# One load of 128 partitions issued as two, of 120 and of 8, at the start of a retention and Fourier-mix kernel

## The chip, the cores and the metric

The kernel runs on one core of a Trainium2 chip. The metric is the device time of one execution in microseconds; the median of three runs before the change is 243.88 us, with a lowest of 243.7 and a highest of 243.89. The core has a matrix engine (PE, with its weight loads shown as PEld), a vector engine (DVE), a scalar engine (ACT), a general engine (POOL) and a queue engine that only issues transfers (SP). Transfers run on 16 DMA engines that all queues share.

## The reference, cut to what matters

Inputs are `q`, `k` and `v` of 4 batches, 8 heads, 768 positions and 64 columns, and two weight matrices of 512 x 2048 and 2048 x 512. The first half is a linear attention with a decay per head, the second a two-dimensional Fourier mix with a normed feed-forward part:

```python
state = gamma * state + k[:, :, t] (outer) v[:, :, t]        # for every position t
y[:, :, t] = q[:, :, t] @ state / sqrt(64)
x = y, heads side by side                                    # 4 x 768 x 512
u = x + real(fft(fft(x, axis=1), axis=2))
ch = relu(norm(u) @ w_ch1) @ w_ch2
out = u + ch                                                 # 4 x 768 x 512, float32
```

## The kernel before

The work goes batch by batch, and inside a batch by four pairs of heads, in the order of `PAIR_ORDER`. For each pair, `load_unit` (line 162 on) issues three loads of 384 KB on SP's queue, `q`, `k` and `v`, each to one tile of 128 partitions x 2 heads x 6 chunks x 64 columns in float32 (the issue itself is line 171). Pairs are counted from 0, so the first batch's fourth `k` is the load that is called k3 here; its neighbours are q3 and v3. The `q` of the first batch is read in runs of 1536 bytes, `k` and `v` in runs of 256 bytes, twelve to a partition.

For the first batch all twelve loads are issued at the very start, back to back. `first_units` then writes out the order of the first batch by hand. Per pair: POOL casts `q` (`q0_unit`, line 403) and scales `k` (`k0_unit`, lines 412 and 415, both halves on POOL for the first three pairs; for the fourth pair line 412 on POOL and line 419 on ACT), and casts `v` (`v0_unit`, line 428; for the fourth pair the second half is cast by DVE on line 432). PE transposes `q` and `k` (line 444), ACT copies the results out (lines 452 and 455), PE makes the masked products (line 469), DVE masks them (line 476), PE makes the states of the chunks (line 491), DVE scans them (line 500), and PE adds up the output (lines 515 and 531), which ACT writes to the batch's `x` (line 544). Then come DVE's folds (lines 684 and 694), the Fourier products (lines 741, 854, 858) and the feed-forward part (lines 978, 961 and 1000).

Between the cast of q3 and the scaling of k3, POOL issues the first of eight weight transfers (`w1_unit`, line 1154); the other seven (lines 1154 and 1161) follow right behind the cast of v3. `filler` (line 157) puts matmuls on zeros into PE's stream. The second batch's loads wait for the seventh weight transfer and for a matmul of the first batch's feed-forward part.

The order on each engine has two sources. In the first batch every instruction is tied to the one before it on its engine by `pin`, so its order is that of `first_units`. Behind it, the units of all streams are sorted by hand-set due times in `emit`; from then until the last batch only POOL's order in the first stretch is tied:

```python
            if e[0] < 1.0:
                behind()
                pin(None if e[0] < 0.05 else ["Pool", "GpSimd"])
            elif e[0] > B - 1:
                pin()
```

Where nothing is tied, the framework's planner orders the instructions of an engine when the kernel is built, from the order of the code and from its own estimate of when each is ready. The four zero fills of `qt_zeros` (lines 270 and 271) belong to that part: the code has them as one unit.

Of the kernel before, what the change touches and what calls it, by code (L numbers as in the profile page):

```python
# [18 lines left out]
P = 128  # L19
# [30 lines left out]
def kernel(  # L50
# [9 lines left out]
    nc = tc.nc  # L60
# [103 lines left out]
    def load_unit(b, i, after=None):  # L164
        def run():
            h0 = 2 * PAIR_ORDER[i]
            for name, src in srcs.items():
                t = inp.tile([P, 2, NCH, D], f32, tag="in32", name=f"{name}32")
                rows = "h (p c) d -> p h c d" if b < NPE and name == "q" else \
                    "h (c p) d -> p h c d"  # L170
                dma = nc.sync.dma_start(t, src[b, h0:h0 + 2].rearrange(rows, p=P))  # L171
                if after is not None:
                    for x in (w_dma[after].ins, lb[0]["mm"].ins):
                        tc.add_manual_dep(dma.ins, x.name,
                                          mybir.DependencyInfo(mybir.DependencyClass.Sync,
                                                               mybir.DependencyReason.DATA),
                                          reason="loads in turn")
                if b > 1:
                    tc.add_manual_dep(dma.ins, a_of[b - 1, 1].ins.name,
                                      mybir.DependencyInfo(mybir.DependencyClass.Sync,  # L180
                                                           mybir.DependencyReason.DATA),
                                      reason="loads behind the transposes")
                in_of[name, b, i] = t
        return run
# [152 lines left out]
    for j in range(2):  # L337
        x = const.tile([P, NCH, 2, XW], f16, tag=f"x16_{j}", name=f"x16_{j}")
# [5 lines left out]
        t = const.tile([P, 257], f32, tag=f"qn_{j}", name=f"qn_{j}", padded_shape=[P, 260])  # L344
# [1020 lines left out]
```

## Time and profile before

| | |
|---|---|
| median of three runs | 243.88 us (243.7 to 243.89) |
| the profiled execution's own time | 244.0 us |
| its span | 241.8 us |
| granted TensorE clock | 1.0 throughout |
| PE busy | 230.9 us, 95% of the span |
| DVE busy | 193.0 us, 80% |
| ACT busy | 126.5 us, 52% |
| POOL busy | 87.1 us, 36% |
| loads on line 171 | 48, of 384 KB each |

The span is the profiled execution from its first to its last instruction; 2.2 us of the execution's own time lie around it. An engine's row in a timeline gives the start in us, the length in us, the engine, the line, the operation and what it writes and reads; a bracket behind it gives the idle time before it and what ended that. A chain of work is followed back from the last instruction, at each step to what released it. In a row of stretches, each engine has its busy time and, in brackets, how many instructions it began; the last three figures are PE's clock, the mean busy share of the 16 DMA engines (packets that overlap on an engine count twice, so that it can go over 1) and GB/s.

### The profile page before, as it was taken

How to read it: one execution, taken by the hardware profiler on the slowest of the kernel's cores; microseconds unless marked ns; L12 is line 12 of the kernel's file. 1: busy time of each engine (PE TensorE's matmuls, PEld its weight loads, DVE VectorE, ACT ScalarE, POOL GpSimd, SP SyncE). 2: the span in 40 equal slices, each digit the busy share in tenths (PEclk: the TensorE clock that was granted, in tenths of full speed). 3: DMA queues.
4: the chain of work that ended last, by engine and by line, in shares of the span. 5: the costliest groups of instructions: out<-in, count | busy, mean ns of one | idle time of the engine just before them, and what ended most of it. 6: DMA issues, size and time to landing. Idle time of an engine off the chain costs nothing.

```text
span 241.8 us, 5656 instructions
## 1 busy us (share of the span) xinstructions
PE 230.9 (95%) x2160; PEld 155.8 (64%) x2160; DVE 193.0 (80%) x478; ACT 126.5 (52%) x280; POOL 87.1 (36%) x150
## 2 busy tenths in 40 slices
PE   6797899999999999999999999999999999999995
PEld 2354568956676655665567546565567458998884
DVE  8998957898897888996787677899985856768264
ACT  8798669588775435662237522742247305253340
POOL 6667600465600058691000553690000602240302
PEclk9999999999999999999999999999999999999999
DMA  7999999799999567999999758787110141131202
GB/s 172 252 265 146 201 200 202 173 246 236 291 222 228 97 146 167 169 201 126 261 274 222 138 118 234 128 111 173 43 46 0 26 130 43 24 110 24 87 0 89
DMA packets 99466, 36.41 MB, mean 151 GB/s; under 512 B 89840, under 2 KB 96624, under 8 KB 99440
## 3 DMA queue, kind: packets, MB, share of 16 engines
q1 hardware_dynamic: 95072, 31.79, 63.4%
q0 software_dynamic: 4224, 4.19, 10.8%
q8 instruction: 17, 0.28, 0.5%
q10 hardware_dynamic: 144, 0.07, 0.1%
q14 instruction: 9, 0.07, 0.1%
HBM read 27.26 MB, written 6.29 MB: 139 GB/s over the span
## 4 chain that ended last, share of the span: by engine, by line
PE 76%; DVE 6%; SPq 4%; POOL 4%; DMA 3%; ACT 3%; issue 2%; POOLq 0%; ACTq 0%
PE psc L1000 22%; PE psh L961 19%; PE psh L1042 9%; PE psc L1113 7%; SPq L171 4%; PE ps L741 4%; PE wkA L605 3%; DMA q<-in_q_dram 3%; PE psh L978 3%; PE wkY L659 2%; PE wkY L655 2%; PE pq L838 1%; PE wkK L624 1%; PE tq L561 1%; POOL u L877 1%
## 5 line engine op out<-in xcount | busy, mean ns | idle before, releaser
L1000 PE MATMUL psc<-w,ht 128*128 128x512 f16 x288 | 68.3, 379 | 0.0
L961 PE MATMUL psh<-unT,w 128*128 128x384 f16 x320 | 59.5, 326 | 0.0
L875 POOL TENSOR_TENSOR u<-u,x 128x256 f32<-128x256 f32 x21 | 13.5, 643 | 104.9 <-DVE u L845 95.7
L1000 PEld LDWEIGHTS <-ht 128*128 128x128 f16 x288 | 27.1, 98 | 25.7 <-issue 0.2
L961 PEld LDWEIGHTS <-w 128*128 128x128 f16 x320 | 29.9, 98 | 16.0 <-issue 0.6
L965 ACT ACTIVATE ht<-psh 128x384 f16<-128x384 f32 x46 | 22.3, 489 | 24.2 <-PE psh L961 24.0
L608 DVE TENSOR_TENSOR atm<-wkA,maskp 128x512 f16<-128x512 f32 x36 | 23.8, 683 | 1.0 <-PE wkA L605 1.0
L1042 PE MATMUL psh<-unT,w 128*128 128x256 f16 x192 | 21.5, 272 | 0.0
L967 DVE TENSOR_SCALAR ht<-psh 128x384 f16<-128x384 f32 x34 | 18.7, 549 | 2.1 <-PE psh L961 2.1
L895 DVE BATCH_NORM_STATS2 bst<-u 128x6 f32<-128x512 f32 x21 | 14.6, 693 | 7.2 <-POOL u L877 7.1
L1042 PEld LDWEIGHTS <-w 128*128 128x128 f16 x192 | 18.7, 98 | 2.2
L1047 ACT ACTIVATE ht<-psh 128x512 f16<-128x512 f32 x21 | 12.5, 597 | 13.1 <-PE psh L1042 8.2
L634 DVE SCALAR_TENSOR_TENSOR s<-s,gk,wkK 128x128 f16<-128x128 f16 x48 | 16.4, 342 | 2.7 <-ACT s L630 1.9
L1004 DVE SCALAR_TENSOR_TENSOR ob<-psc,stats,u 128x512 f32<-128x512 f32 x18 | 13.4, 744 | 4.9 <-PE psc L1000 4.8
L667 ACT ACTIVATE x<-wkY,gexp 128x384 f16<-128x384 f32 x24 | 12.8, 581 | 8.3 <-PE wkY L659 8.3
L900 ACT ACTIVATE un<-u,stats 128x512 f16<-128x512 f32 x15 | 10.8, 721 | 10.6 <-DVE stats L896 7.1
L388 POOL TENSOR_SCALAR kd<-k,gexp 128x384 f16<-128x384 f32 x24 | 13.9, 590 | 3.8 <-DMA k<-in_k_dram 3.8
L157 PE MATMUL wps<-ht 128*128 128x512 f16 x40 | 12.6, 418 | 2.2 <-POOL ht L208 2.2
L877 POOL TENSOR_TENSOR u<-u,x 128x256 f32<-128x256 f32 x21 | 13.3, 635 | 3.3 <-DVE u L848 2.1
L605 PE MATMUL wkA<-qTz,kT 128*128 128x256 f16 x72 | 13.4, 273 | 0.1
L978 PE MATMUL psh<-unT,w 128*128 128x128 f16 x192 | 11.5, 219 | 0.1
L978 PEld LDWEIGHTS <-w 128*128 128x128 f16 x192 | 11.0, 98 | 0.7 <-issue 0.5
(191 smaller groups left out, 415.6 us busy)
## 6 DMA issues: line engine op xcount, KB each, us to landing
q<-in_q_dram SPq DMA_DIRECT2D x16, 384.0 KB, 6.3
k<-in_k_dram SPq DMA_DIRECT2D x16, 384.0 KB, 5.7
v<-in_v_dram SPq DMA_DIRECT2D x16, 384.0 KB, 6.3
out_dram<-ob SPq DMA_DIRECT2D x18, 256.0 KB, 2.7
w<-in_moe_w_ch_dram POOLq DMA_DIRECT2D x8, 512.0 KB, 10.9
out_dram<-o SPq DMA_DIRECT2D x2, 512.0 KB, 2.9
out_dram<-o SPq DMA_DIRECT2D x3, 128.0 KB, 1.8
unT<-un SPq DMA_TRANSPOSE x15, 2.5
```

The costliest lines, as they stand in the source:

```text
L605: mm = nc.tensor.matmul(wk[:, c2], st["kT"][:, c, :], st["qT"][:, :, c, :], start=True, stop=True)
L608: nc.vector.tensor_tensor(out=st["atm"][:, 2 * part:2 * part + 2], in0=wk, in1=maskp[:, PAIR_ORDER[i]].unsqueeze(1).to_broadcast([P, 2, 2, ...
L634: nc.vector.scalar_tensor_tensor(out=s16[:, c], in0=s16[:, c - 1], scalar=gk2[:, hp:hp + 1], in1=wk[:, c - c0], op0=ALU.mult, op1=ALU.add)
L877: nc.gpsimd.tensor_tensor(out=u[:, kb, 256:512], in0=u[:, kb, 256:512], in1=x[:, kb, 1, 257:1:-1], op=ALU.add)
L895: nc.vector.bn_stats(bst, u[:, kb, :])
L961: nc.tensor.matmul(psh, w116[:, cb, fb * P:(fb + 1) * P], unT[:, cb, rt * 384:(rt + 1) * 384], start=(cb == 0), stop=(cb == 3))
L965: nc.scalar.activation(ht16[:, fb, :], psh, AF.Relu, bias=0.0, scale=-1.0)
L967: nc.vector.tensor_scalar(out=ht16[:, fb, :], in0=psh, scalar1=-1.0, scalar2=0.0, op0=ALU.mult, op1=ALU.max)
L978: mm = nc.tensor.matmul(psh[:, f], w116[:, cb, fb * P:(fb + 1) * P], unT[:, cb, kb * P:(kb + 1) * P], start=(cb == 0), stop=(cb == 3))
L1000: nc.tensor.matmul(psc, ht16[:, fb, rb3 * P:(rb3 + 1) * P], w216[:, fb, :], start=(fb == 0), stop=(fb == NFB - 1))
L1042: nc.tensor.matmul(psh[:, t], w116[:, cb, fb * P:(fb + 1) * P], unT[:, cb, p * 256:(p + 1) * 256], start=(cb == 0), stop=(cb == 3))
L1113: nc.tensor.matmul(ps[:, c0:c1], lh(f), rh(f)[:, c0:c1], start=first and f == 0, stop=last and f == 7, skip_group_check=True)
```

## The change

The load k3, and no other, is issued as two transfers on the same queue, one behind the other: partitions 0 to 119, then partitions 120 to 127. Both write the same tile, so whoever reads the tile waits for both. Nothing else differs.

```diff
                 t = inp.tile([P, 2, NCH, D], f32, tag="in32", name=f"{name}32")
                 rows = "h (p c) d -> p h c d" if b < NPE and name == "q" else \
                     "h (c p) d -> p h c d"
-                dma = nc.sync.dma_start(t, src[b, h0:h0 + 2].rearrange(rows, p=P))
+                x = src[b, h0:h0 + 2].rearrange(rows, p=P)
+                cut = 120 if (b, i, name) == (0, 3, "k") else P
+                dma = nc.sync.dma_start(t[0:cut], x[0:cut])
+                if cut < P:
+                    nc.sync.dma_start(t[cut:P], x[cut:P])
```

## The prediction

> **What bounds the kernel now.** I read the page first: shares of busy time, then the chain that ended last.
>
> ```profile
> PE 230.9 (95%) x2160; PEld 155.8 (64%) x2160; DVE 193.0 (80%) x478; ACT 126.5 (52%) x280; POOL 87.1 (36%) x150
> PE 76%; DVE 6%; SPq 4%; POOL 4%; DMA 3%; ACT 3%; issue 2%; POOLq 0%; ACTq 0%
> ```
>
> PE bounds the kernel as a whole, but the change sits in the first 23 us, and there the chain runs through transfers. So I asked for the chain in order of time around the fourth pair.
>
> ```profile
> 11.71 7.67 DMA q<-in_q_dram
> ...
> 19.55 0.83 POOL q16z L403
> 20.38 0.90 POOL w L1154
> 21.29 0.04 issue
> 21.33 0.98 POOL kd L412
> 22.31 0.13 issue
> 22.44 0.49 PE tq L444 x6
> ```
>
> The reader should see that the chain waits for q3, not for k3: q3 lands at 11.71 + 7.67 = 19.38, POOL casts it, issues a weight transfer, and only then comes to k3. The DMA issues, asked for one at a time, give k3's and v3's landings (us from issue to landing is the last figure), and the timeline gives their starts, POOL's row for v3 and PE's and DVE's rows that need v3.
>
> ```profile
> 14.41 0.47 SPq L171 DMA_DIRECT2D k<-in_k_dram  x1
> 15.00 1.46 SPq L171 DMA_DIRECT2D v<-in_v_dram  x1
> k<-in_k_dram SPq DMA_DIRECT2D x1, 384.0 KB, 6.7
> v<-in_v_dram SPq DMA_DIRECT2D x1, 384.0 KB, 7.5
> 22.53 0.55 POOL L428 TENSOR_SCALAR v<-v 128x384 f16<-128x384 f32 x1 [0.23 <-DMA v<-in_v_dram]
> 23.28 0.54 DVE L432 CAST v<-v 128x384 f16<-128x384 f32 x1
> 24.31 0.47 PE L491 MATMUL wkK<-v,kd 128*64 128x64 f16 x10
> ```
>
> k3 lands at 14.41 + 6.7 = 21.11, which is 0.18 us before POOL is free for it (21.29). v3 lands at 15.00 + 7.5 = 22.5. Last I cut the tail of these loads into stretches; the last two figures are the busy share of the 16 DMA engines and GB/s. A row of the DMA queues for 16.0 to 17.5 us goes with it.
>
> ```profile
> 20.00:20.50 0.50, 0.06 (x1) 0.06 (x2) 0.50 (x2) 0.50 (x3) 0.50 (x2) 1.00 1.31 211
> 21.00:21.50 0.50, 0.50 (x6) 0.26 (x5) 0.50 (x2) 0.50 (x1) 0.46 (x2) 1.00 0.13 34
> 21.50:22.00 0.50, 0.45 (x13) 0.32 (x11) 0.50 (x2) 0.50 (x2) 0.50 (x1) 1.00 0.07 16
> q8 instruction: 1, 0.02, 5.5%
> q1 hardware_dynamic: 66, 0.02, 7.5%
> ```
>
> A share of 0.07 of 16 engines is 1.1 engines: at 21 us nearly all engines are done with all twelve loads, and one is still working through its parts of k3 and v3. The last row is the load queue from 21.0 to 22.0: 66 packets of 256 bytes in 1 us, one every 15.2 ns, one engine's pace. One instruction packet at 16.0 to 17.5 us held one engine for 0.055 x 16 x 1.5 = 1.3 us, which is about the lag. That it is the same engine is my inference; which of the 16 it is, these views don't say.
>
> **The change, part by part.** Three things change: SP issues one more transfer, k3's rows are dealt to the engines in two portions, and the readers of k3 wait for two transfers.
>
> The issue. k3's issue takes 0.47 us and v3's 1.46 us. The nearest rows for an issue of 8 partitions are the k issues, 0.45 to 0.47 us; plus the gap of 0.04 between issues, v3 is issued about 0.5 us later, at 15.5. Its data starts to move behind k3's, at about 19 us or later, so 0.5 us or even another 1.5 us (if the extra issue has to wait as v3's does) hides in the 3.5 us in between. SP issues nothing else until 44.58. Cost 0. Without that cover it would be 0.5 us on v3, of which 24.31 - 23.82 = 0.49 us is slack at PE: DVE's cast of v3's half ends at 23.82, and PE needs it at 24.31.
>
> The portions. Eight rows are 8 x 12 = 96 packets. If a portion of 120 still gives its engines 8 rows each and the 8 rows go one to an engine, an engine with a ninth row has 12 packets more, 12 x 15.2 ns = 0.18 us. Three cases by which engine is the late one: it gets a ninth row, and k3 lands at 21.11 + 0.18 = 21.29, just as POOL comes free; it has eight as before, and k3 lands at 21.11; it has none, and k3 lands with the others, before 20.9, when the share has dropped. The scaling starts at 21.33 in the last two and by 21.42 in the first (0.13 from landing to start, below). Cost 0 to 0.09 us. An early landing brings nothing, because POOL is still at q3 and the weight issue until 21.29, and these follow q3, which is queued ahead of k3 and isn't touched. v3 moves with it: 0.18 later at worst, which is inside the 0.49 us; or, if the late engine is relieved of 96 packets, to about 21.3, when POOL casts it at 22.34 in place of 22.53. Then seven weight issues come 0.19 us earlier. That is worth nothing: the second batch's loads that wait for a weight transfer wait last for a PE matmul of L978 (2.0 us by the waits of SP's queue), and no row of PE's waits names a weight transfer.
>
> [...]
>
> The waits. POOL's line 412 and ACT's line 419 get a second transfer to wait for. The nearest rows: the first pair's scaling, which has a separate semaphore instruction, starts at 6.09 after a landing at 1.32 + 4.6 = 5.92, 0.17 us; the second pair's, without one, starts at 10.68 after 5.04 + 5.6 = 10.64, 0.04 us. So a second wait costs 0.13 us when it comes last and nearer to the 0.04 of a queue step when both are long over. POOL's is on the chain: +0.05 us, between 0 and 0.13. Behind the waiting instruction on POOL stand the cast of v3 and seven weight issues, all covered as above. On ACT, line 419 starts at 21.68 behind a copy that runs until 21.79; it ends at 22.30 and POOL's half at 22.31, and PE needs both. So 0.05 us on ACT falls beside POOL's 0.05 and not on top; without POOL's it would count in full.
>
> The sum: 0 + 0 to 0.09 + 0.05, of which I take 0.05 for likeliest, since two of the three cases cost nothing. The profiled execution's 244.0 becomes 244.05; that execution is 0.12 us above the median of 243.88, so the forecast is 243.9 to 243.95 against the runs, and I name 243.95.
>
> **The rivals.** First, the planner. Behind the first batch most of the order is the planner's, made from estimated times, and an added transfer can shift its estimates. The profile shows that it moves things: the unit of four zero fills stands scattered.
>
> ```profile
> 39.18 0.38 DVE L270 MEMSET qTz<- 64x384 uint32 x1
> 39.67 0.38 DVE L271 MEMSET qTz<- 64x384 uint32 x1
> 40.08 0.69 DVE L987 TENSOR_SCALAR ht<-psh 128x512 f16<-128x512 f32 x1
> 42.45 0.38 DVE L270 MEMSET qTz<- 64x384 uint32 x1
> 44.22 0.38 DVE L271 MEMSET qTz<- 64x384 uint32 x1
> ```
>
> Two of them lie on the chain from 39.18 to 40.05, 0.87 us. One such placement more, or one fewer, is what a new order would move: 243.9 + 0.9 = 244.8, or 243.9 - 0.9 = 243.0. For it: the scattered fills. Against: everything up to the end of the first batch is pinned on every engine, so a shift that is equal for all that follows leaves the order alone. Of a tuned order and a new one, more new ones are worse.
>
> Second, on the slow side by one mechanism: the 8 rows are not pipelined behind the 120 but land a full transfer later. The nearest row of a small transfer is the 64 KB store, 1.6 us from issue to landing. Then k3 lands at 21.11 + 1.6 = 22.7, POOL scales it at 22.75 in place of 21.33, and with 1.42 us more the time is 245.3. It decides from a landing of 21.29 on, and is over 0.2% from 21.8. Against: v3 lands 1.4 us after k3, and its 96 packets at 15.2 ns are 1.46 us, so a transfer behind another pays no start of its own. [...]
>
> Third, the change does nothing, because k3 is not what POOL waits for; that is my forecast's own ground.
>
> **How the numbers follow.** 0.2% of 243.9 is 0.49 us, about what a measurement can tell from no change. No change beyond that, with the order kept or changed without effect: 0.40, its own range 243.8 to 244.2. Planner, slower: 0.26; planner, faster: 0.24; late second portion: 0.10. So faster 0.24, same 0.40, slower 0.36. The range reaches from the fast planner case to the late portion, with a little below: 242.9 to 245.3, leaving out the cases with several displaced instructions, some 0.15.
>
> **What would show it.** In the changed kernel: two issues near 14.41 and 14.93 and v3's by 16.7; k3's second landing at or before 21.3; the scaling on L412 at 21.33 to 21.42 behind the weight issue and not behind a transfer; the transposes within 0.1 us of 22.44. A scaling that waits for a transfer makes the second rival right. An order on DVE, ACT or PE behind 40 us that differs, such as the fills' places, makes the first right. A q3 that lands at another time than 19.38 would make the whole reading wrong.

## The result, and the profile after

The changed kernel takes 245.24 us (median of four runs, 245.04 to 245.46) beside 243.81 us for the kernel before (243.7 to 243.89): a ratio of 1.0055, with a 95% interval of 1.004 to 1.007. It is slower by 0.55%. The time lies inside the predicted range, on its slow side, but by luck: neither the forecast (no change) nor either of the mechanisms given for a slower kernel is what happened. The profiled execution, the longest of the four, takes 245.46 us, with a span of 243.1 us where the one before has 241.8.

The page of the changed kernel, first busy time and then the chain's shares:

```profile
PE 230.9 (95%) x2160; PEld 155.9 (64%) x2160; DVE 192.6 (79%) x478; ACT 126.5 (52%) x280; POOL 86.6 (36%) x150
PE 68%; DMA 8%; DVE 7%; ACT 5%; SPq 4%; POOL 4%; issue 2%; POOLq 0%; ACTq 0%; DVEq 0%
```

PE works exactly as long as before, 230.9 us, so the 1.3 us are idle time, and the chain's share of transfers is 8% where it was 3%. On every engine the order of the working instructions is the one of before; new are the second transfer and a wait on POOL, and DVE has one wait fewer. The chain around the fourth pair, in order of time, shows the first part of the loss:

```profile
11.57 8.52 DMA q<-in_q_dram
...
20.27 0.84 POOL q16z L407
...
21.16 0.52 PE tq L448 x6
...
21.70 0.63 ACT qTz L456
...
22.40 0.62 ACT kd L423
...
23.16 0.49 PE tq L448 x6
```

The load of q3 is issued 0.14 us earlier than before and takes 8.52 us in place of 7.67. It lands at 20.10 and not at 19.38, although it stands ahead of k3 in the queue. All that follows is late by this: PE transposes k3 at 23.16 in place of 22.44, which is 0.72 us. PE's distance from its times of before then stays: 0.72 until 61 us, 0.78 behind that, and 0.86 from 146 us to its last matmul. What makes the two small additions is open.

SP's timeline and POOL's row for k3 show that k3 itself is later still:

```profile
14.28 0.52 SPq L173 DMA_DIRECT2D k<-in_k_dram  x1
14.85 1.43 SPq L175 DMA_DIRECT2D k<-in_k_dram  x1
16.40 0.39 SPq L173 DMA_DIRECT2D v<-in_v_dram  x1
22.41 0.58 POOL L416 TENSOR_SCALAR kd<-k,gexp 128x384 f16<-128x384 f32 x1 [0.41 <-DMA k<-in_k_dram]
```

The portion of 120 partitions lands at 22.31 (21.11 to 21.14 before), the portion of 8 at 20.92, ahead of it. POOL now does wait for k3. Its half, 0.58 us long where it was 0.97 before, ends at 22.99 and ACT's, which stands behind the copy of q3's transposes, at 23.02. So q3 and k3 delay PE side by side: as an estimate from these rows, either late landing alone would have cost most of the 0.72 us. Why are q3 and k3 late? The row of the load queue between 18.0 and 20.5 us gives packets, MB, and the time that they took as a share of 16 engines. First the kernel before, then the changed one:

```profile
q1 hardware_dynamic: 2144, 0.56, 133.2%
```

```profile
q1 hardware_dynamic: 1574, 0.41, 130.2%
```

The engines are as full as before, but each packet takes longer: 1.332 x 16 x 2500 ns / 2144 = 24.9 ns before, 1.302 x 16 x 2500 / 1574 = 33.1 ns after. Between 17.5 and 20.5 us the queue holds what is left of q3 and the two portions of k3. One engine is behind the others in both kernels: q3 has 16 landings, read here as one for each engine, of which fifteen are there by 18.12 us before and by 18.17 after, and the last at 19.38 and 20.10. That engine still has some of q3's runs of 1536 bytes to bring, one behind the other. Those that began between 18.0 and 19.0 us took 70 ns each before and 131 ns after, on average. The last of them is over at 18.83 before and at 19.26 after, and the landing comes 0.55 us behind it before and 0.84 after. This is the late landing of q3.

The second part of the loss is at the end. The waits of SP's queue on transfers in the last 6 us, before and then after:

```profile
SPq L1360 <- DMA out_dram<-o: 0.8, 3, 0.3
```

```profile
SPq L1364 <- DMA out_dram<-o: 1.2, 1, 1.2
```

SP ends the program by waiting for the last transfers of all queues, in a fixed order of semaphores, 0.06 us for each wait that is already fulfilled. The transfers issued by SP and ACT take eight semaphores in turn (numbers 101 to 105 and 108 to 110 in the trace). Before, the last store is on the eighth, so the three waits that stop are the last three: the last store lands at 240.89, and SP is through at 240.97, 0.08 us later. With one transfer more every later one moves on by one semaphore, and the last store is on the first of the eight. SP stops there for 1.2 us, until 241.79 for a landing at 241.78, and then works through the seven waits behind it, all long fulfilled, until 242.29: 0.51 us. That is 0.43 us more.

The sum: 0.72 + 0.06 + 0.08 + 0.43 = 1.29 of the 1.31 us in the span. Another 0.15 us of the 1.46 between the two profiled executions lie around the span; nothing in the trace shows where.

### The profile page after: what moved, and what is told of

Its sections match the earlier page's. It is cut to its first block, busy times and chain, and to the rows that moved or that the text cites. A ratio compares the mean times of both kernels' runs of the same rounds, so it can differ in the third digit from the quotient of the medians.

```text
span 243.1 us, 5657 instructions
## 1 busy us (share of the span) xinstructions
PE 230.9 (95%) x2160; PEld 155.9 (64%) x2160; DVE 192.6 (79%) x478; ACT 126.5 (52%) x280; POOL 86.6 (36%) x150
## 4 chain that ended last, share of the span: by engine, by line
PE 68%; DMA 8%; DVE 7%; ACT 5%; SPq 4%; POOL 4%; issue 2%; POOLq 0%; ACTq 0%; DVEq 0%
PE psc L1004 19%; PE psh L965 19%; PE psh L1046 9%; PE psc L1117 7%; DMA q<-in_q_dram 6%; SPq L173 4%; PE ps L745 4%; PE wkA L609 3%; DMA k<-in_k_dram 3%; PE wkY L663 2%; PE wkY L659 1%; POOL u L881 1%; PE pq L842 1%; DVE bst L899 1%; PE wkK L628 1%
```

## The experiments

Each is the kernel before with the edit shown, unless it says "the change". Ratios are to the kernel before on the same chip, with 95% intervals.

### Other cuts of k3

**Two transfers of all 128 partitions, one for each head:**

```diff
-                dma = nc.sync.dma_start(t, src[b, h0:h0 + 2].rearrange(rows, p=P))
+                x = src[b, h0:h0 + 2].rearrange(rows, p=P)
+                if (b, i, name) == (0, 3, "k"):
+                    nc.sync.dma_start(t[:, 0], x[:, 0])
+                    dma = nc.sync.dma_start(t[:, 1], x[:, 1])
+                else:
+                    dma = nc.sync.dma_start(t, x)
```

> k3 again as two transfers on one queue, but cut by head: each has all 128 partitions and half the bytes. My theory: the start loses time because the portion of 120 partitions is dealt to the DMA engines in another way and its packets get slower (33 to 35 ns against 25 ns), not because there are two transfers. So here q3 lands at 19.4 as before, POOL scales k3 at 21.3 to 21.4, PE's transposes of it start at 22.4 to 22.5, and only the end is longer by 0.43 us, since there is one transfer more and the last store's semaphore is again the first that the closing waits come to: 243.8 + 0.4 = 244.2 to 244.3. Rival, any second transfer costs the start (issue, second wait): q3 or k3 late by 0.5 us or more and 245.0 to 245.3.

**64 and 64 partitions** (`cut = 64`):

> k3 cut at 64 partitions: two portions of 64. If packets get slower whenever a portion is dealt in another way than a whole 128 (rows that one engine writes lie elsewhere), they are slower here too, q3 lands after 19.6 and the time is 244.7 to 245.5. If only a portion that leaves engines out is slow, q3 lands at 19.4 and the time is 244.2 to 244.3, the longer end alone.

**112 and 16 partitions** (`cut = 112`):

> k3 cut at 112 partitions: portions of 112 and of 16, both multiples of 16, so that no engine need be left out, but with 7 rows to an engine in the first. If the way of dealing is what slows the packets, this is like the change: q3 at 19.8 to 20.3 and 244.8 to 245.5. If it is the engine left out, or the uneven share, q3 lands at 19.4 and the time is 244.2 to 244.3.

Measured, with the mean of a packet from the load queue's row of 18.0 to 20.5 us, worked out as above:

| k3 cut into | mean packet | q3 lands | k3's last landing | PE behind at k3's transposes | at the end | ratio |
|---|---|---|---|---|---|---|
| one (before) | 24.9 ns | 19.38 | 21.14 | 0 | 0 | 1 |
| 2 x 128, by head | 24.7 ns | 19.43 | 21.16 | 0.37 | 0.68 | 1.0023 (1.0015 to 1.0032) |
| 112 + 16 | 28.4 ns | 19.72 | 21.77 | 0.34 | 1.24 | 1.0062 (1.0044 to 1.0081) |
| 64 + 64 | 31.7 ns | 20.11 | 22.19 | 1.28 | 1.85 | 1.0066 (1.0048 to 1.0084) |
| 120 + 8 (the change) | 33.1 ns | 20.10 | 22.31 | 0.72 | 0.86 | 1.0055 (1.004 to 1.007) |

Packets, landings and PE's times are those of one profiled execution each. How far such a figure strays by itself is shown by the kernels whose packets of 256 bytes keep the old pace: before, the cut by heads, and three kernels further below (one small transfer more behind v3, 128 bytes more, 24 fillers fewer) have q3 between 19.23 and 19.59, k3's last landing between 20.99 and 21.25, and PE up to 0.37 behind at k3's transposes. So the packets and k3's landing of 112 and 16 are clear of the spread, its 0.34 us at PE is not.

The rows for the two by head, for 64 and 64, and for 112 and 16:

```profile
q1 hardware_dynamic: 2139, 0.55, 132.1%
```

```profile
q1 hardware_dynamic: 1710, 0.45, 135.5%
```

```profile
q1 hardware_dynamic: 1900, 0.49, 135.0%
```

So it is not that there are two transfers, nor that an engine gets nothing. A cut by heads leaves packets and landings as they were; a cut of the partitions slows them, and so it is with 64 and 64 and with 112 and 16, where the trace has 16 landings for every portion. All three kernels have the longer end as well (0.4 us).

Three of PE's figures have more in them than q3 and k3. With 112 and 16, PE is 0.34 us behind until 57 us; it then waits twice, at 57.1 and at 62.6 us, for POOL's scaling of the second batch's `k` (0.47 and 0.45 us), and POOL waits for that load, which is not cut. With 64 and 64, PE's clock is granted at 0.50 to 0.54 from 21 to 24 us, after PE was idle for 1.71 us in its wait for q3; in the changed kernel's profiled run the clock stays at 1.00 behind an idle time of 1.64 us. The low clock came in two of the six runs with 64 and 64 (246.46, which is the profiled one, and 246.55 us); the other four take 245.24 to 245.72.

The cut by heads holds by its time: 0.54 us over before, of which the longer end gives 0.43. Its profiled run, the slowest of eleven, is late at the start all the same: k3 is there, POOL starts on it at 21.39, but takes longer for the same instruction than before (0.97).

```profile
21.39 1.37 POOL L417 TENSOR_SCALAR kd<-k,gexp 128x384 f16<-128x384 f32 x1
```

That makes PE 0.37 us late, and another 0.30 come on at 62 us, in a wait for the second batch's `k` as above. Why POOL took 0.40 longer was not tested; the row of the same instruction is anywhere between 0.58 and 1.37 us in these kernels.

### The end alone

**One small transfer more, behind the second batch's loads:**

```diff
+            if (b, i) == (1, 3):
+                spare = const.tile([P, 1, 16], f32, tag="spare", name="spare")
+                for n in range(1):
+                    more = nc.sync.dma_start(spare[:, n], q[0, 0, 0:P, 0:16])
...
```

The lines left out tie it behind the load before it.

> The kernel before, with k3 whole and one small transfer more (128 partitions of 64 bytes to a tile that nothing reads), behind the second batch's loads. My theory of the end: transfers take eight semaphores in turn, the closing waits go through them in a fixed order, and one transfer more turns the turn, so that the last store sits at the second wait in place of the last and the waits behind it come after its landing, 7 x 0.065 = 0.45 us: 243.8 + 0.43 = 244.2, with PE's instructions where they were (offset under 0.15 us). Rival, the end of the changed kernel is longer because its last store itself landed later: no change here, 243.8.

It came out faster: 243.72 us beside 244.19, a ratio of 0.9986 (0.9977 to 0.9994). Its end is longer as expected, 0.52 us from the last landing to SP's last wait. But ten of the twelve first loads land earlier, k3 at 18.63 in place of 21.14, 40 us before the added transfer is issued (59.35). The tile `spare`, 64 bytes on each partition, was the last in its pool, and every tile behind it had moved by 64 bytes. So this run doesn't test the end alone, and asks for two others: the transfer without the move, and the move without the transfer.

**One small transfer more, with the tile behind all others,** so that no other tile moves:

```diff
     stt = pool("stt", 2)
+    spp = pool("spp", 1)
...
+            if (b, i) == (0, 3):
+                spare = spp.tile([P, 16], f32, tag="spare", name="spare")
+                for n in range(1):
+                    nc.sync.dma_start(spare[16 * n:16 * n + 16], q[0, 0, 0:16, 0:16])
```

> The kernel before with one transfer of 1 KB (16 rows of 64 B into a tile that nothing reads, behind all other tiles, so that no other tile moves) right behind v3. Theory of the closing waits: the first loads land as before and PE is within 0.1 of before, but the last store is on the first of the eight semaphores, and SP waits through the other seven behind it: 0.51 from the last landing to SP's drain instead of 0.08, span 242.2, ratio 1.001 to 1.0025. Theory that the number of transfers costs nothing at the end: span 241.8, ratio 1.000.

Measured: 244.58 us beside 244.17, ratio 1.0021 (1.0011 to 1.0031), span 242.2. PE is 0.09 us ahead of before at its last matmul; the last store lands at 240.80 on the first semaphore, and SP is through at 241.31. SP's wait has the changed kernel's form:

```profile
SPq L1365 <- DMA out_dram<-o: 1.2, 1, 1.2
```

A transfer of 1 KB, issued at 16.5 us, that nobody reads costs 0.4 us, all of it in the closing waits. The theory held.

**The change, and seven transfers of 1 KB behind v3,** into the same kind of tile, which turn the semaphores back to where they were:

```diff
+                for n in range(7):
+                    nc.sync.dma_start(spare[16 * n:16 * n + 16], q[0, 0, 0:16, 0:16])
```

> The change with seven transfers of 1 KB (16 rows of 64 B into a tile that nothing reads, behind all other tiles) right behind v3, so that there are eight transfers more than before and the last store is again on the last of the eight semaphores. Theory of two parts: q3 lands at 20.1 and PE stays 0.86 behind, but the time from the last landing to the end is 0.08 instead of 0.51: ratio 1.003 to 1.004, 0.4 us below the change. Theory that the end comes from something else than the turn of the semaphores: 0.5 from landing to end, ratio 1.005 to 1.006.

Measured: 245.19 us, ratio 1.0047 (1.0031 to 1.0062). The last store lands at 241.96 on the eighth semaphore and SP is through at 242.05, 0.09 us later, with three short stops as before the change:

```profile
SPq L1369 <- DMA out_dram<-o: 0.8, 3, 0.3
```

The end is as expected. The sum isn't. q3 lands at 19.80 and not at 20.1, and PE is 0.63 us behind at k3's transposes, less than in the change; but another 0.34 come on at 62 us, where PE waits for POOL's scaling of the second batch's `k` and where the change loses 0.06. So PE ends 1.04 us behind and not 0.86, and the last exchange between the engines took 0.1 us longer. Most of the 0.42 us won at the end was lost again, so the time alone would not have shown it; the two places in the trace do.

### The same cut at other places

**The second pair's k,** at 7 to 11 us: `cut = 120 if (b, i, name) == (0, 1, "k") else P`.

> The 120 and 8 rows made of the second pair's k instead of the fourth's, at a time when no instruction packet holds an engine. Theory that dealing fewer than 128 rows slows every engine that it meets: the 256 B packets take 30 to 35 ns for some 2.5 us from 7 us on, and as one transfer queues behind the other all landings from k1 on are 0.6 to 0.9 later, q3's last too (20.1), PE 0.6 to 0.9 behind from the fourth pair on, and 0.43 at the end: ratio 1.004 to 1.0055. Theory that it costs only the one engine that the instruction packet holds: landings as before but for k1's by 0.2, PE within 0.1, 0.43 at the end: ratio 1.0018.

Measured: 245.3 us, ratio 1.0047 (1.0032 to 1.0061). The load queue from 8.5 to 11.0 us has 24.8 ns a packet before and 31.4 with this cut:

```profile
q1 hardware_dynamic: 2177, 0.55, 135.2%
```

```profile
q1 hardware_dynamic: 1685, 0.43, 132.4%
```

k1's last landing moves from 10.59 to 11.61 (here it is the portion of 8 that lands last; the 120 are there at 11.04), v1's from 12.32 to 12.97, and q3's from 19.38 to 19.94; PE is 1.08 behind at the second pair's k, 0.56 at the fourth's, and 0.39 at its end. With the closing waits the span is 0.8 us longer; the rest of the time lost lies around the span. No packet of instructions falls in this window, so the slowing needs no engine that one holds. The first theory held, though not in every size: k1's landing moved by more than the 0.6 to 0.9 it named, q3's and PE by a little less.

**The fourth pair's v** instead of its k: `cut = 120 if (b, i, name) == (0, 3, "v") else P`.

> The 120 and 8 rows made of the fourth pair's v instead of its k. Theory that the slow dealing meets what is in the air at the same time: the portions start when most engines are through with k3, at 19.4 to 19.9, so q3's last landing stays at 19.4, k3's last moves from 21.1 to 21.4 to 21.9, v3's others from 21.5 to 22.2; PE behind by 0.2 to 0.7, and 0.43 at the end: ratio 1.0025 to 1.0045. Theory that a cut transfer slows what is queued ahead of it from its issue on: q3 at 20.1 as in the change, PE 0.86 behind, ratio 1.005 to 1.006.

Measured: 245.02 us, ratio 1.004 (1.0024 to 1.0055). Packets stay at 25 ns until 19.0 us and then take 28 to 36, until 21.0. q3 lands at 19.70, 0.32 later: only the end of its last engine's work meets the portions. k3 lands at 21.95, 0.81 later, and POOL waits for it. PE is 0.54 behind at the fourth pair and 0.84 at the end (the profiled run, 245.64 us, is the longest of six; the others take 244.91 to 245.28). So the portions slow what is in the air at the same time, and not whatever is queued ahead of them. The expectation that q3 would not move at all was too strict, by the one engine that still had some of it.

### The 64 bytes

**64 bytes more, and no transfer:** the padding of the last tile ahead of the loads' tiles grows.

```diff
-        t = const.tile([P, 257], f32, tag=f"qn_{j}", name=f"qn_{j}", padded_shape=[P, 260])
+        t = const.tile([P, 257], f32, tag=f"qn_{j}", name=f"qn_{j}", padded_shape=[P, 260 + 16 * j])
```

> The kernel before with 64 B more behind the tile qn_1 and no further transfer, so that every tile behind it, those of the loads first, lies 64 B higher: they start on a multiple of 256 B, where before they start 192 B past one. Theory of the address: the loads' 256 B packets take 18 ns as in e4_one_more instead of 25, k3 lands at 18.6 instead of 21.14, PE is ahead by 0.86 to the end, and the closing waits stay at 0.08: span 240.9, ratio 0.996 to 0.997. Theory that e4_one_more's gain came from its transfer or from a shift of the planner: packets 25 ns, span 241.8, ratio 1.000.

**128 bytes more** (`260 + 32 * j`):

> The kernel before with 128 B more at the same place: the tiles of the loads start 64 B past a multiple of 256 B. Theory of the address: each 256 B packet still lies across a boundary, packets 25 ns, times as before, ratio 0.999 to 1.001. Theory that any other place is better than the one before (a clash of two tiles, say): packets 18 ns, ratio 0.996 to 0.997.

Measured: with 64 bytes 243.08 us beside 244.13, ratio 0.996 (0.9946 to 0.9974), span 240.9; with 128 bytes 244.08 us, ratio 1.0002 (0.9993 to 1.0011), span 242.0. The kernel with 64 bytes is thus faster than both the kernel before and the change. What the core's transfers moved from 1.0 to 20.5 us, in 40 equal slices of GB/s, before and with 64 bytes:

```profile
GB/s 0 22 91 331 362 292 289 237 220 218 218 245 258 362 295 263 218 216 218 218 221 251 312 335 290 234 216 219 218 217 273 231 338 298 281 234 225 223 218 210
```

```profile
GB/s 0 22 123 299 357 290 288 287 290 288 254 226 380 308 290 287 290 289 304 343 380 295 290 287 283 290 290 330 343 283 265 262 285 292 187 39 36 34 18 24
```

The long stretches at about 218 GB/s are those in which the runs of 256 bytes of `k` and `v` are loaded alone; with 64 bytes they go at about 288, and each packet takes 17.9 ns (4.0 to 5.8 us) in place of 25.4 (5.5 to 6.5 us). With 128 bytes they are at 216 to 220 again. The tiles of the loads begin at byte 95680 of a partition before, 192 bytes past a multiple of 256, so that every run of 256 bytes crosses one; at 95744 they begin on one, and at 95808 they are 64 past one. So the loads are slower in both kernels whose tiles start off the multiple, and 64 past is no faster than 192 past: 26.3 and 25.0 ns a packet from 4.5 to 6.5 us. Of a load, the edits move only the address that is written, not the one that is read; by what mechanism the start costs time was not shown.

PE ends only 0.93 us earlier though k3's last landing is 2 us earlier (19.16), because the start now hangs on ACT. The chain:

```profile
20.35 0.68 ACT qTz L452
21.03 0.53 ACT kd L419
...
21.69 0.50 PE tq L444 x6
```

**The change with the 64 bytes:**

> The change together with the 64 B of e9_pad64. Both theories have the closing waits at 0.51 instead of 0.08, +0.43. Theory that the dealing of the rows to the engines slows the packets by itself: 256 B packets at 18 to 20 us take over 22 ns, q3 lands 0.5 or more behind e9_pad64's, and the time is 0.6 to 1.2 us over e9_pad64: ratio to the kernel before 0.9985 to 1.0015. Theory that it slows them only where each packet crosses a boundary: 18 ns, q3 at 17.4 as in e9_pad64, and the time is e9_pad64's with 0.43 more: ratio 0.998 to 0.9985.

Measured: 243.81 us, ratio 0.9984 (0.9974 to 0.9993), 0.73 us over the 64 bytes alone; the spans differ by 0.48 (240.87 and 241.35). The load queue from 17.0 to 18.0 us, with the 64 bytes alone (18.3 ns a packet) and with the change on top (26.2 ns):

```profile
q1 hardware_dynamic: 970, 0.26, 110.8%
```

```profile
q1 hardware_dynamic: 783, 0.20, 128.2%
```

The slowing is there at this address too, and q3 lands at 18.59 in place of 17.77. So the first theory holds in what it says of packets. The time doesn't decide, since the ratio lies at the edge that the two theories share, and the first theory's came out only in part: PE is 0.71 late for q3, but transposes k3 at 21.65 as in the kernel with 64 bytes alone (21.69), and stays level to the end. The late q3 is covered by ACT, whose half of k3's scaling ends at 21.51 here and at 21.55 there, and the closing waits' 0.43 us are nearly all of the difference in the span. Of the 0.66 us between the two profiled executions another 0.18 lie around the span, as 0.15 do in the change.

### The late engine

> The kernel before without 24 of the filler matmuls on wps in the first pairs (the result is not touched), so that PE's program is 48 instructions shorter at that place and the 16 KB instruction packet that lies at 16.05 comes at another time. Theory that this packet is what makes one engine bring its part of q3 1.3 us behind the others: q3's last landing is 18.1 to 18.3 in place of 19.38, and another transfer has the late engine. Theory that the late engine is always that of q3's last rows: 19.4 as before. The time itself says nothing here, since the granted clock may change.

The edit leaves out 24 matmuls of `filler`, up to the third pair; its one run takes 244.32 us. The instruction packet came at 16.75 and not at 16.05, still within q3's stretch, and q3 landed at 19.23 with the other engines done by 17.93. Both theories allow that landing. The trace's single packets say more. In the kernel before, the instruction packet is over at 17.367 us, and at 17.353 a run of q3 begins that takes 178 ns; from it on the late engine brings its last runs one behind the other. With the fillers left out the packet ends at 17.884 and that run begins at 17.870. In the change, with the 64 bytes, and with both, it again begins 14 ns before the packet's end (17.200, 16.112 and 15.396). The trace doesn't name the engine, but the late runs wait for the end of the instruction packet wherever that lies, so it is the packet that makes this engine late. With the 64 bytes alone a second engine is late too (17.27, where fourteen are done by 15.72), and why is open.

## Why the prediction was right and wrong

**The issue** was right. SP issues the portions at 14.28 and 14.85 and v3 at 16.40, inside the bound of 16.7; the long issue, v3's before (1.46 us), is now that of the portion of 8 (1.43 us), and v3's takes 0.39. It cost nothing.

**The portions** are where the prediction failed. It priced them at 0 to 0.09 us by counting packets on one engine at its old pace, and closed the case with "these follow q3, which is queued ahead of k3 and isn't touched". Both halves fail. The pace is not fixed: it went from 24.9 to 33.1 ns a packet. And a place ahead in the queue did not protect q3: fifteen of its 16 landings were there by 18.17 and those of k3 began at 19.83, before the sixteenth of q3 at 20.10. The term measured 0.72 us at PE's transposes, from q3 and k3 together. The prediction did name this place as the one to look at: a q3 that lands at another time than 19.38 would make the reading wrong, and it landed at 20.10. That the late engine is the one that the instruction packet held, which it called an inference, the late engine's runs above bear out.

How the rows were dealt shows in the landings: k3 has 16 before, and in the change there are 15 for the portion of 120, from 19.83 to 22.31, and 8 for the portion of 8, from 20.22 to 20.92. Read as one for each engine, the late engine is one of the 15, whose last landing is 1.66 us behind the fourteenth (20.65), and not of the 8. Its part of k3 then kept eight rows, if the 15 share the 120 evenly, which is an estimate: the second of the prediction's three cases, priced at 0.

**The waits** were bounded by 0 and 0.13 us. Their two rows were misread in part, because the landings were added up from times rounded to 0.1 us: by the trace the first pair's landing is at 5.93 and the second's at 10.59, so that the scaling starts 0.16 and 0.09 us behind them and not 0.17 and 0.04. In the change POOL starts 0.10 behind k3's landing, so the second wait, long over by then, cost about 0.01. It lies beside ACT's half and is not in the sum.

**v3** lands at 23.53, a full 1.07 us later than before. The prediction's slack for it was 0.49 us; it was not used up only because PE itself was 0.72 later.

**The planner** left the order alone, as the forecast had it. Half of the chance went to that rival.

**The late second portion** did not come, though its sign did: the scaling waits for a transfer (0.41 us idle), but for the portion of 120. The 8 rows land 1.4 us before it. That this rival's 245.3 us is near the measured 245.24, and is the upper end of the range, is chance: the range held by a mechanism that wasn't there. With the second pair's k cut in the same way, the 8 rows did land last, 0.57 us behind the 120. Nor is there a full transfer's time, for which the prediction took 1.6 us, between the portions in the change: 20.92 for the 8 rows is 0.27 behind the landing of the 120 on all engines but the late one (20.65).

**What the sum left out** is the end. The prediction took the change to sit in the first 23 us. One transfer more changes which semaphore the last store is on, and that cost 0.43 us, by itself nearly the 0.49 us that it called measurable. The profile of before shows a part of it, SP's closing waits on the last stores with three stops, the longest 0.3 us; that one more transfer moves the last store to the front of the turn has to be worked out from the semaphores.

Open is why a cut of the partitions slows packets. The trace names no engine, and no run here moved the same rows to other partitions, so whether it is their place or their number that counts was not tested. Nor does any run tell the writing side from the reading side: a cut of the partitions may also change which rows of `k` in memory an engine reads.

## What to carry to other kernels

A load on all 128 partitions should be cut along its free dimension if it has to be cut: here halves by head cost the transfers nothing, while 112 + 16, 64 + 64 and 120 + 8 made the mean packet in the air take 14, 27 and 33% longer, and with 120 + 8 those of an earlier transfer too (q3's runs of 1536 bytes, 131 ns in place of 70). Count the transfers of a kernel against the turn of its semaphores: here one transfer more cost 0.43 us at the end in the change, and seven more on top of it won 0.42 back there. And look at the byte at which the tile of a load with short runs begins: 64 bytes of padding, and nothing else, won 0.4% here. A single profiled run is not the median: PE's lag at the end had up to 0.9 us in it that came from waits for other loads.

## What the runs showed that was not expected

- Loads in runs of 256 bytes went at about 218 GB/s into tiles that begin 192 or 64 bytes past a multiple of 256, and at about 288 GB/s into tiles that begin on one.
- A transfer of 1 KB that nothing reads cost 0.41 us of 244.2, over 220 us after it was issued.
- The 17 packets of instructions of 16 KB in the kernel before took 0.93 to 1.53 us each. The first, of 1.31 us, ended at 17.37, and the engine whose runs then waited for its end landed its part of q3 at 19.38, 1.26 us behind the others.
- One tile of 64 bytes, declared for an experiment, moved all tiles behind it and made the kernel faster by 0.14% in spite of a longer end. An experiment that declares a tile should put it behind all others.
